# Scalar loads on another queue and a later second projection in the last chunk of an attention and gated feed-forward kernel

## The chip, the cores and the metric

The kernel runs on one core of a Trainium2 chip. The metric is the device time of one execution in microseconds (us); the times below are those of the kernel before, and the median of its runs is what the changed kernel is held against. The engines are named as in the profile: PE is TensorE (matmuls; PEld are its weight loads), DVE is VectorE, ACT is ScalarE, POOL is GpSimd, and SP is SyncE, which issues nearly all DMAs.

## The reference

Attention with a sliding window of 128 and 4 sink positions for 4 x 8 heads of 768 positions by 64, followed by a gated feed-forward block over all 3072 rows:

```python
def _attn_ref(q, k, v, n_sink, window):
    scores = scale * np.matmul(q, k.transpose(0, 1, 3, 2))
    keep = is_sink | in_window          # pos < n_sink, 0 <= rel < window
    scores = np.where(keep, scores, -1000000000.0)
    scores = scores - np.max(scores, axis=-1, keepdims=True)
    a = np.exp(scores)
    a = a / (np.sum(a, axis=-1, keepdims=True) + 1e-09)
    return np.matmul(a, v).astype(np.float32)

def _moe_ref(x, w_gate, w_val, w_out):
    gate = 1.0 / (1.0 + np.exp(-(x @ w_gate)))
    val = x @ w_val
    return (gate * val @ w_out).astype(np.float32)
```

`x` has 512 columns, `w_gate` and `w_val` are 512 x 1536, `w_out` is 1536 x 512. `n_sink` and `window` are two integers that the kernel reads from memory.

## The kernel before

**Work.** Attention runs in 96 units: one head, two tiles of 128 rows each. The first 16 units (`PLAIN`) multiply in plain float32; the later ones, and the feed-forward, split each operand into a high and a low part and sum three products of them. The weights arrive as pairs of 32-bit words and are decoded on DVE, ACT and POOL into high and low parts (`decode`). The low part of `w_out` (`wlo`) is written back to memory (`wol_d`) and read again per block into `wol`, two buffers in turn.

**Feed-forward.** The rows are cut into eight chunks (`MT`); the last one (`ci == 7`) has three tiles, 384 rows. For each of 12 blocks `f` of 128 hidden columns `feed_part` (line 1089) emits: the up projections, 12 matmuls into one PSUM tile `m` for the gate (weights `wgh`, `wgl`) and 12 into another for the value (`wvh`, `wvl`); `th` (a tanh on ACT, then a product on DVE); `gh` (its high part, on ACT or DVE) and `gl` (the rest, on POOL or DVE, helper `rest`); and the second projection `down`, nine matmuls `o<-woh,gh`, `o<-wol,gh`, `o<-woh,gl` for three output tiles, which accumulate over the blocks. After block 11 ACT halves each `o` into an output tile and SP sends it out.

**Order.** Nothing is placed by hand. Every step is an `Op` with a priority and one or more engines that could do it (`ways`). `Plan.run` walks them through a small model of the five queues (Q is SP's) and writes out one fixed order for each engine; an engine then works strictly through its row of instructions and stops at a wait. On PE, where nothing else is ready in the first stretch, the planner puts warming matmuls `m<-ident`. Priorities on PE are `pe = 10000 + ci + f / 12`: the gate of block `f` at `pe`, the value at `pe + 0.3 / 12`, `down` at `pe + 0.5 / 12`. So `down` of block `f` ranks ahead of both up projections of block `f + 1`, although it is passed over while its inputs are not surely there.

**Scalars.** `n_sink` and `window` are loaded by two DMAs at the head of SP's row (line 571). DVE turns them into the masks `am`, which the first unit needs.

**The way out.** A count of unusual inputs (`count<-bad,one` on PE, `flag` and `total` on DVE, lines 1197 to 1201) is loaded by every engine (`TENSOR_LOAD`, line 1203); if it is above zero, a slow general version runs, else every engine branches past that code (line 1204) to the end of the program.

Of the kernel before, what the change touches and what calls it, by code (L numbers as in the profile page):

```python
# [24 lines left out]
MT = ((2,2),(2,),(3,),(3,),(3,),(3,),(3,),(3,))  # L25
# [8 lines left out]
SCALP = -0.5  # L34
# [399 lines left out]
def kernel(  # L434
# [20 lines left out]
    DO = w_out.shape[1]  # L455
    NC = DM // 128
    NF = DF // 128
# [20 lines left out]
    plan = Plan()  # L478

    class InOrder:  # L480
# [9 lines left out]
    PE, V, A, G, Q = (  # L490
        InOrder(e) for e in (nc.tensor, nc.vector, nc.scalar, nc.gpsimd, nc.sync)
    )

    def vec(cols, fast=False):
        return 80 + (0.95 if fast else 1.25) * cols

    def act(cols, psum=False):
        return (48 if psum else 90) + 0.84 * cols

    def pool(cols):  # L500
        return 250 + 2.2 * cols

    def mac(cols):
        return max(cols * 13 / 12 / 2.4, 104.5) + 2.5

    def dma(prio, ns, fn, r=(), w=()):
        plan.op(prio, [("Q", 460, fn)], r, w, dma=ns)

    def copy(prio, cols, out, in_, r, w, psum=False):

        plan.op(
            prio,
            [
                ("A", act(cols, psum), lambda: A.copy(out=out(), in_=in_())),
                ("V", vec(cols, not psum), lambda: V.tensor_copy(out=out(), in_=in_())),
            ],
            r, w,
        )

    def rest(prio, cols, out, in0, in1, r, w, psum=False):  # L520

        plan.op(
            prio,
            [
                (
                    "G", pool(cols), lambda: G.tensor_tensor(
                        out=out(), in0=in0(), in1=in1().bitcast(F32), op=ALU.subtract
                    ),
                ),
                (  # L530
                    "V", vec(cols), lambda: V.tensor_tensor(
                        out=out(), in0=in0(), in1=in1().bitcast(F32), op=ALU.subtract
                    ),
                ),
            ][1 if psum else 0 :],
            r, w,
        )
# [13 lines left out]
    def tile(shape, dtype, tag, bufs, pool=None):  # L551
        return Tile(pool or p1, shape, dtype, tag, bufs)
# [15 lines left out]
    nums = tile([128, 10], I32, "nums", 1)  # L568
    mk = tile([128, 704], F32, "wst", BUFS["wst"], p2)

    for i, s in enumerate((n_sink, window)):
        dma(
            SCALP, 56.0, lambda i=i, s=s: Q.dma_start(
                out=nums()[:, 2 * i : 2 * i + 2],
                in_=s.bitcast(I32).rearrange("(o x) -> o x", o=1).broadcast_to([128, 2]),
            ), w=[(nums, i)],
        )

    def scalars():
# [481 lines left out]
    def feed(ci, g, parts):  # L1061

        O = []
        for p, T in enumerate(parts):
            for _ in range(T):
                j = len(O)
                O.append(
                    tile([128, DO], F32, f"o{j}", 1, ps)
                    if j < 3 else tile([128, DO], F32, "a", BUFS["a"], ps)
                )  # L1070
        for f in range(NF):
            j0 = 0
            for p, T in enumerate(parts):
                feed_part(ci, g, p if len(parts) > 1 else None, j0, T, f, O[j0 : j0 + T])
                j0 += T
        for j, acc in enumerate(O):
            ot = (
                tile([128, DO], F32, "qkT", BUFS["turned"]) if ci == len(MT) - 1 and j == 2
                else tile([128, DO], F32, "w2", BUFS["w2"])
            )  # L1080
            r = (g + j) * 128
            plan.op(
                -1000.0 + ci + 1,
                [("A", act(DO, True), lambda acc=acc, ot=ot: A.mul(out=ot(), in_=acc(), mul=0.5))],
                [acc], [ot],
            )
            dma(ci, 728.0, lambda ot=ot, r=r: Q.dma_start(out=out[r : r + 128], in_=ot()), [ot])

    def feed_part(ci, g, p, j0, T, f, O):
        W = T * 128  # L1090
        r0 = (g + j0) % RING
        xs = slice(r0 * 128, r0 * 128 + W)
        pr = -1000.0 + ci + f / NF
        pe = 10000.0 + ci + f / NF
        wgh, wgl, wvh, wvl, woh = wres[f]
        wol = tile([128, DO], F32R, f"wol{f % 2 if p is None else p}", BUFS["wol"])
        dma(
            pr, 728.0, lambda: Q.dma_start(out=wol().bitcast(F32), in_=wol_d[f]),
            [(WOL, f)] + ([] if f else [(XH, (NC - 1, r0 + T - 1))]), [wol, (LOADS, p)],
        )  # L1100
        th = tile([128, W], F32, "th", BUFS["th"])
        gh = tile([128, W], F32R, "gh", BUFS["g"])
        gl = tile([128, W], F32R, "gl", BUFS["g"])
        for i, (hi, lo) in enumerate(((wgh, wgl), (wvh, wvl))):
            m = Tile(MS, None, F32, "m", BUFS["m"])
            todo = [
                (c, j, w, x)
                for c in range(NC)
                for j, (w, x) in enumerate(((hi, XH), (hi, XL), (lo, XH)))
            ]  # L1110
            for s in range(UPS):
                part = todo[s * 12 // UPS : (s + 1) * 12 // UPS]

                def up(part=part, m=m):
                    for c, j, w, x in part:
                        PE.matmul(
                            m()[:, 0:W], lhsT=w()[:, c], rhs=x()[:, c, xs],
                            start=c == 0 and j == 0, stop=c == NC - 1 and j == 2,
                        )

                plan.op(
                    pe + 0.3 * i / NF, [("PE", len(part) * mac(W), up)],
                    [hi, lo] + [(x, (c, r0 + t)) for c, _, _, x in part for t in range(T)],
                    [m] if s else [m, th, (GROUPS, p)] if i == 0 else [m, gh, gl, (GROUPS, p)],
                )
            if i == 0:
                plan.op(
                    pr, [("A", act(W, True), lambda m=m: A.activation(
                        out=th(), in_=m()[:, 0:W], func=AF.Tanh, scale=0.5
                    ))],  # L1130
                    [m], [th],
                )
            else:
                plan.op(
                    pr, [("V", vec(W), lambda m=m: V.scalar_tensor_tensor(
                        out=th(), in0=th(), scalar=1.0, in1=m()[:, 0:W], op0=ALU.add,
                        op1=ALU.mult,
                    ))],
                    [m], [th],
                )  # L1140
        copy(pr, W, gh, th, [th], [gh])
        rest(pr, W, gl, th, gh, [th, gh], [gl])
        for j in range(T):

            def down(j=j):
                ts = slice(j * 128, j * 128 + 128)
                for i, (x, w) in enumerate(((gh, woh()[:, 0]), (gh, wol()), (gl, woh()[:, 0]))):
                    PE.matmul(
                        O[j](), lhsT=x()[:, ts], rhs=w,
                        start=f == 0 and i == 0, stop=f == NF - 1 and i == 2,  # L1150
                    )

            plan.op(
                pe + 0.5 / NF, [("PE", 3 * mac(DO), down)], [gh, gl, woh, wol], [O[j]]
            )

    decoding = iter(range(3 * NF))
# [95 lines left out]
```

## Time and profile before

| | us |
|---|---|
| runs | 796.38, 807.41, 798.26 |
| median | 798.26 |
| profiled execution | 798.38 |
| its span, first to last instruction | 796.7 |
| PE busy in the span | 773.8 (97%) |
| DVE, ACT, POOL busy | 513.4, 403.2, 437.5 |

The profiled execution has 1.7 us outside its span (798.38 less 796.7). All instructions of the plan are recorded under one line, 488, so they are told apart by the tiles that they write and read (`out<-in`). A busy share near 100% on PE says that PE is where the time is, but it includes the warming matmuls and stretches at a lower clock.

### The profile page before, as it was taken

What the parts mean: (1) busy time and instruction counts of PE and PEld (TensorE: products, weight loads), DVE (VectorE), ACT (ScalarE), POOL (GpSimd) and SP (SyncE); (2) the same over time, 40 slices, a digit from 0 to 9 for tenths busy, and PEclk for the clock granted to TensorE, in tenths of its full rate; (3) what the DMA queues carried; (4) which work ended last, traced back from release to release, by engine and by line L of the source; (5) the groups of instructions that cost most, each with busy time, mean ns of one, the idle gap of its engine ahead of it and who ended that gap; (6) DMA issues with size and microseconds to landing.
All of it is one profiled execution on the core that took longest, in us unless ns stands there. A gap on an engine that the chain in (4) does not pass through costs nothing. (4 is left out here: it accounts for less than half of the span.)

```text
span 796.7 us, 14763 instructions
## 1 busy us (share of the span) xinstructions
PE 773.8 (97%) x4540; PEld 702.8 (88%) x4540; DVE 513.4 (64%) x1550; ACT 403.2 (51%) x1190; POOL 437.5 (55%) x602
## 2 busy tenths in 40 slices
PE   7999999999999999999999999999999999999996
PEld 5677798878999999998999999999999999999995
DVE  5787798998799988899871388885861331111110
ACT  4786777766767767676640256664740210011001
POOL 3676798887667778668761267673751221111211
PEclk8999999999999999999999999999999999999999
DMA  5667777763645544444441235343311121113111
GB/s 162 198 190 207 191 213 253 231 201 115 192 126 151 149 107 122 119 116 112 142 113 40 57 104 133 104 129 111 92 45 42 41 79 40 40 40 92 39 42 57
DMA packets 98421, 94.33 MB, mean 118 GB/s; under 512 B 43168, under 2 KB 77984, under 8 KB 98336
## 3 DMA queue, kind: packets, MB, share of 16 engines
q1 hardware_dynamic: 98336, 93.32, 41.1%
q8 instruction: 38, 0.62, 0.3%
q14 instruction: 47, 0.39, 0.1%
HBM read 83.85 MB, written 9.44 MB: 117 GB/s over the span
## 5 line engine op out<-in xcount | busy, mean ns | idle before, releaser
L488 DVE SCALAR_TENSOR_TENSOR th<-th,m 128x384 f32<-128x384 f32 (+1 forms) x108 | 54.6, 505 | 184.3 <-PE m L488 182.9
L488 POOL TENSOR_TENSOR gl<-th,gh 128x384 fp32r<-128x384 f32 (+1 forms) x65 | 65.5, 1008 | 195.4 <-DVE gh L488 183.0
L488 ACT ACTIVATE th<-m 128x384 f32<-128x384 f32 (+1 forms) x108 | 49.1, 454 | 209.4 <-PE m L488 207.5
L488 POOL TENSOR_SCALAR_AFFINE_SELECT wt<-wt 128x512 fp32r<-128x512 f32 (+3 forms) x192 | 121.5, 633 | 42.6 <-DVE wt L488 24.2
L488 PE MATMUL m<-XH,wvh 128*128 128x384 f32 (+1 forms) x432 | 140.1, 324 | 0.4 <-ACT th L488 0.4
L488 PE MATMUL m<-XH,wgh 128*128 128x384 f32 (+1 forms) x432 | 140.3, 325 | 0.0
L488 PE MATMUL m<-XH,wvl 128*128 128x384 f32 (+1 forms) x432 | 137.7, 319 | 0.0
L488 PE MATMUL m<-XL,wvh 128*128 128x384 f32 (+1 forms) x432 | 137.6, 319 | 0.0
L488 PE MATMUL m<-XH,wgl 128*128 128x384 f32 (+1 forms) x432 | 137.5, 318 | 0.0
L488 PE MATMUL m<-XL,wgh 128*128 128x384 f32 (+1 forms) x432 | 137.3, 318 | 0.0
L488 PE MATMUL o<-woh,gh 128*128 128x512 f32 x276 | 113.0, 409 | 1.0 <-DVE total L1201 1.0
L488 PE MATMUL o<-woh,gl 128*128 128x512 f32 x276 | 109.5, 397 | 2.2 <-DVE gl L488 1.6
L488 PE MATMUL o<-wol,gh 128*128 128x512 f32 x276 | 108.8, 394 | 2.5 <-DMA wol<-wol_d 2.5
L488 ACT ACTIVATE P<-P,negm_all 128x132 f32<-128x132 f32 x192 | 77.2, 402 | 30.5 <-DVE negm_all L488 27.0
L488 PEld LDWEIGHTS m<-XH,wvh 128*128 128x128 f32 x432 | 81.7, 189 | 3.3 <-ACT th L488 0.6
L488 PEld LDWEIGHTS m<-XH,wgh 128*128 128x128 f32 x432 | 81.4, 189 | 2.1 <-issue 0.2
L488 PEld LDWEIGHTS m<-XL,wvh 128*128 128x128 f32 x432 | 81.8, 189 | 1.5
L488 PEld LDWEIGHTS m<-XL,wgh 128*128 128x128 f32 x432 | 81.5, 189 | 1.6
L488 PEld LDWEIGHTS m<-XH,wvl 128*128 128x128 f32 x432 | 81.7, 189 | 0.0
L488 PEld LDWEIGHTS m<-XH,wgl 128*128 128x128 f32 x432 | 81.3, 188 | 0.0
L488 PEld LDWEIGHTS o<-woh,gl 128*128 128x128 f32 x276 | 52.0, 188 | 16.6 <-DVE gl L488 3.5
L488 DVE CUSTOM_DVE_ANT_0 P<-a,am 128x132 f32<-128x132 f32 x192 | 56.2, 294 | 11.9 <-PE a L488 2.9
(115 smaller groups left out, 1619.5 us busy)
## 6 DMA issues: line engine op xcount, KB each, us to landing
wol<-wol_d SPq DMA_DIRECT2D x108, 256.0 KB, 2.7
qkT<-in_k_dram SPq DMA_DIRECT2D x120, 99.0 KB, 2.6
qkT<-in_q_dram SPq DMA_DIRECT2D x176, 64.0 KB, 2.4
wst<-in_moe_w_gate_dram SPq DMA_DIRECT2D x12, 512.0 KB, 4.3
wst<-in_moe_w_val_dram SPq DMA_DIRECT2D x12, 512.0 KB, 4.3
wst<-in_moe_w_out_dram SPq DMA_DIRECT2D x12, 512.0 KB, 4.2
vraw<-in_v_dram SPq DMA_DIRECT2D x64, 96.0 KB, 2.3
out_dram<-w SPq DMA_DIRECT2D x23, 256.0 KB, 2.5
```

Of the source, the lines that this page charges most:

```text
L488: return lambda *a, **kw: tc.keep_in_program_order(op(*a, **kw))
```

## The change

The two scalars are loaded by ACT's queue in place of SP's. In the last chunk `down` gets the priority `pe + 1.4 / 12`, which is behind both up projections of the next block (the next value projection is at `pe + 1.3 / 12`). In the last chunk's last block `gl` is computed by DVE alone: the fifth flag of `rest` strikes POOL off the list.

```diff
     for i, s in enumerate((n_sink, window)):
-        dma(
-            SCALP, 56.0, lambda i=i, s=s: Q.dma_start(
+        plan.op(
+            SCALP, [("A", 460, lambda i=i, s=s: A.dma_start(
                 out=nums()[:, 2 * i : 2 * i + 2],
                 in_=s.bitcast(I32).rearrange("(o x) -> o x", o=1).broadcast_to([128, 2]),
-            ), w=[(nums, i)],
+            ))], w=[(nums, i)], dma=56.0,
         )
...
         pe = 10000.0 + ci + f / NF
+        last = ci == len(MT) - 1
...
-        rest(pr, W, gl, th, gh, [th, gh], [gl])
+        rest(pr, W, gl, th, gh, [th, gh], [gl], last and f == NF - 1)
...
-                pe + 0.5 / NF, [("PE", 3 * mac(DO), down)], [gh, gl, woh, wol], [O[j]]
+                pe + (1.4 if last else 0.5) / NF, [("PE", 3 * mac(DO), down)], [gh, gl, woh, wol], [O[j]]
```

Since the planner decides step by step, the two loads' new place alters its choices from the first microseconds on, and the rows of all engines come out in another order along the whole program. Three places follow.

PE at the end of the last chunk, before: the last value projection (block 11), the count, and the `down` of block 11; `down` of block 10 (`woh10`) stands ahead of these rows.

```order
L488 MATMUL m0_90<-XL_83,wvh11_151 128x384
L488 MATMUL m0_90<-XH_82,wvl11_152 128x384
L1197 MATMUL count_10044<-bad_10036,one_10042 1x4
L488 MATMUL o00_9564<-woh11_153,gh1_10014 128x512
L488 MATMUL o00_9564<-wol10_9982,gh1_10014 128x512
L488 MATMUL o00_9564<-woh11_153,gl1_10016 128x512
```

The same place now: the last value projection is followed by the nine matmuls of block 10, of which the first three are shown.

```order
L488 MATMUL m1_91<-XL_83,wvh11_151 128x384
L488 MATMUL m1_91<-XH_82,wvl11_152 128x384
L488 MATMUL o00_9583<-woh10_148,gh1_9971 128x512
L488 MATMUL o00_9583<-wol00_9942,gh1_9971 128x512
L488 MATMUL o00_9583<-woh10_148,gl1_9976 128x512
```

And PE's last rows now: the count has moved behind the last matmul of `down`, directly ahead of the load of `total`.

```order
L488 MATMUL o20_9594<-woh11_153,gh0_10013 128x512
L488 MATMUL o20_9594<-wol10_9984,gh0_10013 128x512
L488 MATMUL o20_9594<-woh11_153,gl0_10018 128x512
L1198 MATMUL count_10046<-bad_10038,one_10044 1x4
L1204 TENSOR_LOAD total_10050
L1205 COMPARE_AND_BRANCH
```

SP at the end, before: the load of `total` stands ahead of the three last output DMAs.

```order
L488 DMA wol10_9982<-wol_d_93 128x512
L1203 TENSOR_LOAD total_10048
L1203 ISA x2
L488 DMA out_0_dram<-w21_10024 128x512
L488 DMA out_0_dram<-w20_10030 128x512
L488 DMA out_0_dram<-qkT2_10033 128x512
```

Now the load of `total` comes behind them.

```order
L488 DMA wol10_9984<-wol_d_93 128x512
L488 DMA out_0_dram<-w21_10026 128x512
L488 DMA out_0_dram<-w20_10032 128x512
L488 DMA out_0_dram<-qkT2_10035 128x512
L1204 TENSOR_LOAD total_10050
L1204 ISA x2
```

ACT at the start, before (`P` are the first units' weights: the rows with `negm_all` are the exponentials, those with `rs` alone as second input scale by the row sums; `w<-wst` begins the decoding of a gate and a value weight block):

```order
L488 ACT_TABLE_LOAD
L488 CAST vsp_84<-w20_190 96x512
L488 ACTIVATE P0_215,rs0_218<-P0_215,negm_all_80 128x132 x2
L488 ACTIVATE P1_230,rs1_234<-P1_230,negm_all_80 128x132
L488 ACTIVATE w21_241<-wst1_205 128x512
L488 ACTIVATE w20_248<-wst2_209 128x512
L488 ACTIVATE P0_215<-P0_215,rs0_218 128x128 x2
```

Now the two scalar loads stand ahead of the table load, and the first weight decoding stands ahead of three of the exponentials.

```order
L488 DMA nums0_156<-in_n_sink_dram 128x2
L488 DMA nums0_156<-in_window_dram 128x2
L488 ACT_TABLE_LOAD
L488 CAST vsp_84<-w20_179 96x512
L488 ACTIVATE P0_219,rs0_226<-P0_219,negm_all_80 128x132
L488 ACTIVATE w21_232<-wst1_196 128x512
L488 ACTIVATE P0_219,rs0_226<-P0_219,negm_all_80 128x132
L488 ACTIVATE P1_230,rs1_241<-P1_230,negm_all_80 128x132
L488 ACTIVATE w20_246<-wst2_200 128x512
L488 ACTIVATE P1_230,rs1_241<-P1_230,negm_all_80 128x132
L488 ACTIVATE P0_219<-P0_219,rs0_226 128x128
```

## Rows read from the trace of the kernel before

**Rows 1.** Busy time of the engines by stretch of the span. Columns: stretch, its length, then busy us (instructions) of PE, PEld, DVE, ACT and POOL, PE's granted clock as a share of full speed, the busy share of the DMA engines, GB/s.

```profile
0.00:50.00 50.00, 43.18 (x227) 31.52 (x228) 35.37 (x130) 32.08 (x93) 29.11 (x52) 0.93 0.61 181
50.00:100.00 50.00, 47.87 (x300) 39.10 (x299) 39.42 (x114) 36.54 (x107) 34.19 (x45) 0.97 0.69 198
100.00:200.00 100.00, 94.60 (x643) 84.61 (x643) 92.22 (x204) 72.06 (x191) 85.54 (x93) 1.00 0.66 201
200.00:786.00 586.00, 585.05 (x3365) 545.89 (x3364) 345.37 (x1101) 260.68 (x798) 287.70 (x414) 1.00 0.34 93
```

**Rows 2.** The timeline of the last blocks: start, duration, engine, line, operation, tiles; in brackets the idle time before it and what ended that. The first two rows are the first matmul of `down` of block 10 and the first of the value projection of block 11; the third is the last of that projection.

```profile
782.02 0.40 PE L488 MATMUL o<-woh,gh 128*128 128x512 f32 x1
...
784.11 0.33 PE L488 MATMUL m<-XH,wvh 128*128 128x384 f32 x1
...
786.05 0.34 PE L488 MATMUL m<-XH,wvl 128*128 128x384 f32 x1
...
786.49 0.56 DVE L488 SCALAR_TENSOR_TENSOR th<-th,m 128x384 f32<-128x384 f32 x1 [7.46 <-PE m L488]
...
787.08 0.36 DVE L488 CAST gh<-th 128x384 fp32r<-128x384 f32 x1
787.36 0.14 DVE L1201 TENSOR_REDUCE total<-flag 1x1 int32<-1x4 int32 x1
787.50 0.51 PE L488 MATMUL o<-woh,gh 128*128 128x512 f32 x1 [0.99 <-DVE total L1201]
787.61 1.00 POOL L488 TENSOR_TENSOR gl<-th,gh 128x384 fp32r<-128x384 f32 x1 [7.38 <-DVE total L1201]
...
788.67 0.50 PE L488 MATMUL o<-woh,gl 128*128 128x512 f32 x1 [0.44 <-POOLq L1204]
...
790.17 0.39 PE L488 MATMUL o<-woh,gl 128*128 128x512 f32 x1
```

**Rows 3.** The forms of `gl` and `gh` on single engines from 580 to 790 us: count, then min/median/max of one in ns, first and last start.

```profile
L488 DVE TENSOR_TENSOR gl<-th,gh x1: 547/547/547, 582.3 to 582.3; 128x384 fp32r<-128x384 f32 x1
...
L488 POOL TENSOR_TENSOR gl<-th,gh x32: 999/1012/1024, 589.9 to 787.6; 128x384 fp32r<-128x384 f32 x32
...
L488 ACT CAST gh<-th x1: 512/512/512, 581.4 to 581.4; 128x384 fp32r<-128x384 f32 x1
```

**Rows 4.** DMA issues of the reloaded low weights: number, size of one, median us from issue to landing.

```profile
wol<-wol_d SPq DMA_DIRECT2D x108, 256.0 KB, 2.7
```

**Rows 5.** The timeline behind PE's last matmul: ACT's last halving and SP's second and third output DMA (SPq is SP's sequencer; the duration is that of the issue).

```profile
790.59 0.60 ACT L488 ACTIVATE qkT<-o 128x512 f32<-128x512 f32 x1
...
790.57 1.54 SPq L488 DMA_DIRECT2D out_dram<-w  x1
792.15 0.43 SPq L488 DMA_DIRECT2D out_dram<-qkT  x1
```

**Rows 6.** All issues of output DMAs: min/median/max ns, first and last start.

```profile
L488 SPq DMA_DIRECT2D out_dram<-w x23: 332/362/1538, 200.1 to 790.6; - x23
```

**Rows 7.** The load of `total` (line 1203) and the branch past the general code (line 1204) on the sequencers: min/median/max ns, first and last start us. The semaphore row of an engine is the first instruction that it runs behind its branch; SP's eight wait for the last DMAs.

```profile
L1203 PEldq TENSOR_LOAD <-total x1: 488/488/488, 788.7 to 788.7; - x1
...
L1204 SPq EVENT_SEMAPHORE  x8: 17/17/17, 794.0 to 795.3; - x8
L1204 DVEq COMPARE_BRANCH  x1: 72/72/72, 788.2 to 788.2; - x1
...
L1204 PEldq COMPARE_BRANCH  x1: 3822/3822/3822, 789.3 to 789.3; - x1
L1204 DVEq EVENT_SEMAPHORE  x1: 21/21/21, 791.0 to 791.0; - x1
...
L1204 SPq COMPARE_BRANCH  x1: 45/45/45, 792.6 to 792.6; - x1
```

**Rows 8.** The timeline of the first 14 us on SP, ACT, DVE and PE.

```profile
0.80 0.40 SPq L488 DMA_DIRECT2D nums<-in_n_sink_dram  x1
1.72 0.56 SPq L488 DMA_DIRECT2D qkT<-in_k_dram  x1
...
4.70 0.24 DVE L488 CAST nums<-nums 128x2 f32<-128x2 uint32 x2 [2.15 <-DMA nums<-in_window_dram]
...
7.13 0.29 DVE L488 CUSTOM_DVE_ANT_0 P<-a,am 128x132 f32<-128x132 f32 x1
...
9.37 0.39 ACT L488 ACTIVATE P<-P,negm_all 128x132 f32<-128x132 f32 x1
11.13 0.70 ACT L488 ACTIVATE w<-wst 128x512 f32<-128x512 f32 x1 [1.28 <-DMA wst<-in_moe_w_gate_dram]
12.55 0.66 ACT L488 ACTIVATE w<-wst 128x512 f32<-128x512 f32 x1 [0.72 <-DMA wst<-in_moe_w_val_dram]
13.11 0.68 ACT L488 ACTIVATE P<-P,rs 128x128 f32<-128x128 f32 x2
...
13.55 0.77 PE L488 MATMUL a<-ident,P 128*128 128x128 f32 x2 [4.05 <-ACT P L488]
```

**Rows 9.** PE alone by stretch (busy us, instructions, granted clock, DMA share, GB/s), and the matmul that ended the wait ahead of the second of them.

```profile
12.40:19.20 6.80, 5.65 (x19) 0.50 0.56 170
...
84.10:87.40 3.30, 3.30 (x14) 0.50 1.05 289
...
83.61 0.50 PE L488 MATMUL o<-wol,gh 128*128 128x512 f32 x1 [1.34 <-DMA wol<-wol_d]
```

## The prediction

> **What bounds the kernel now.** I read the busy times by stretch first [rows 1]. From 200 to 786 us PE is busy for 585.05 of 586.00 us at full clock: there is nothing in that stretch for an order to win, and it holds nearly all of the last chunk. What can be won lies before 200 us, where PE stands still or is slow, and behind 786 us. The end is read from the timeline [rows 2]. The last value projection issues its last matmul at 786.05; matmuls of that width follow each other every 0.175 us here (12 of them from 784.11 to 786.05 and on to 786.22), so PE could go on at 786.22. It starts `down` of block 11 at 787.50, does two matmuls, waits for POOL's `gl` until 788.67 and starts its ninth at 790.17. The reason is a chain with nothing beside it: `th` on DVE until 787.05, `gh` until 787.44, `gl` on POOL from 787.61 to 788.61. The nine matmuls of block 10, from 782.02 to 784.11, were spent earlier. Behind PE's last matmul, which ends at 790.56, ACT halves the last tile (790.59 to 791.19), SP issues its DMA at 792.15 [rows 5], the wait for landings ends at 795.3 [rows 7], and the span at 796.7: 6.1 us from PE's end to the span's end.
>
> **The late second projection.** With `down` of block 10 behind the last value projection, as the order shows, its nine matmuls (784.11 - 782.02 = 2.09 us, or 0.232 each) fill the gap. The work is the same and only the gap goes. Without waits the last matmul would start at 786.22 + 8 x 0.232 = 788.08, against 790.17: **-2.09 us**. This holds if the chain stays under its cover. Counted from 786.22, the cover ends at 2.09 for `gh`, and at 2.09 + 2 x 0.232 = 2.55 for `gl`, which the third matmul needs. `th` is ready at 0.83 (787.05). A step between engines cost 0.17 before (787.44 to 787.61). The planner has put the last `gh` on ACT, 0.51 [rows 3]: 0.83 + 0.17 + 0.51 = 1.51. `gl` on DVE takes 0.55: 1.51 + 0.17 + 0.55 = 2.23, plus a step to PE some 2.35. It fits with 0.2 us to spare. In the other eleven blocks PE had no gap [rows 1], so the later `down` wins nothing there and costs nothing either: POOL's 1.01 [rows 3] has 24 up matmuls (4.2 us) as cover. The slot of `wol` comes free one projection later, but its next reader follows 10 us behind, and a reload takes 2.7 [rows 4].
>
> **The last rest on VectorE.** On POOL `gl` would end at 1.51 + 0.17 + 1.01 = 2.69, against the 2.55 at which it is needed. So this edit is worth 0.1 to 0.3 us of the 2.09, beneath the new cover; alone it would have been worth 1.01 - 0.55 = 0.5.
>
> **The way out.** The order shows two moves that the diff doesn't: the count runs behind PE's last matmul, and SP loads `total` behind its three output DMAs. Let E be the end of PE's last matmul. The DMA chain is the longest before: E + 6.1. One piece of it is odd: the second output DMA took 1.54 us to issue, against a median of 0.36 [rows 6], and held the third from 791.19 to 792.15. If it doesn't come again there, that chain ends at 0.63 (ACT) + 0.03 + 3.15 (792.15 to 795.3) + 1.4 (to the span's end) = E + 5.2, a gain of 0.9. But now the flag starts at E as well. From the end of the last up matmul (786.39) to `total` (787.50) it took 1.1 us before, with `th` and `gh` queued on DVE ahead of parts of it, so 0.5 to 1.1 now. PE's load of it takes 0.49 and its branch took 3.82 [rows 7]; by these the branch is over at E + 1.1 + 0.49 + 0.1 + 3.82 = 5.5, and with 1.4 behind it the end is at E + 6.9, a loss of 0.8. I take less, since of the 3.82 us PE was still multiplying for 1.28 (789.28 to 790.56); 2.5 are left, and DVE took 2.8 from its branch at 788.2 to its next instruction at 791.0. With 2.7 the branch is over at 4.4 and the end is at 5.8. So between -0.9 and +0.8 I choose **-0.3**, from the row of the engine that stood idle when it branched.
>
> [...]
>
> **The scalars on ACT.** SP's row begins 1.72 - 0.80 = 0.92 us earlier [rows 8]. Followed through, little of it arrives. The first reduction on DVE (7.13) waits for the masks, these for the landing of `window` (4.70), and ACT can issue that no earlier than SP did: the first unit's scores are earlier, its exponentials are not. If ACT's issues are slower or the table load behind them delays them, the masks come later, but ACT's next exponentials now stand behind the first weight decoding, which would come to 11.13 - 0.92 = 10.2, so some 1.5 us of lateness (10.2 less the first reduction's 7.13, the exponential's 0.58 and what lies between) is hidden, and what is beyond that costs its full size. Then the new row of ACT: decoding to 10.9, two exponentials at 0.58 each (9.37, and with its read of the sum to 9.85, is such a step; 0.58 is between starts) to 12.1, the second decoding to 12.8, an exponential to 13.4, the scaling: before it began at 13.11 and let PE go at 13.55. So PE's wait of 4.05 us ends at about the same time, 13.7. Between a full gain of 0.92 and a loss as large I take **0**.
>
> **The rest of the program.** The planner's choices differ from there on. PE has the same matmuls and 71 warming ones for 69. Whether PE waits more or less before 200 us can't be read from an order. Its price can be read from one event: PE waited 1.34 us for `wol` at 83.61, and then ran at half clock (1.2 GHz) from 84.1 to 87.4 [rows 9], which loses another 1.65: 3.0 us in all. The other such stretch, 12.4 to 19.2, followed the wait of 4.05 us. So the term is 0, with -3 and +3 as ends: one such event more or less.
>
> **Sum.** -2.09 - 0.3 + 0 + 0 = -2.4 against the profiled execution's own 798.38 (span 796.7 and 1.7 around it), which lies 0.12 above the median of 798.26. That gives **796.0 us**, 0.3% under the median.
>
> **The rivals.**
> *Another waiting of PE is added* (slower than before). The reshuffled row has one more event of the kind at 83.61, in the stretch before 200 us: 796.0 + 3.0 = 799.0, and 1.1 more, 800.1, if the way out is at its bad end as well. It decides from a loss of 2.3 us on, which is what the end gives against the median. For it: in that stretch DVE and POOL are busy for 92.22 and 85.54 of 100 us [rows 1], so a step placed badly isn't made up. Against: the planner's rules are the same.
> *An event goes.* SP's earlier start or another order removes the wait at 13.55 or the one at 83.61 with its half clock: 796.0 - 3.0 = 793.0. For it: all of SP's early loads are 0.92 earlier. Against: ACT's new row, above.
> *The way out eats the gain.* [...] In words of rows: PE's branch takes as long as it did before, though no matmul is left under it.
> *The change doesn't do what it says* (the chain outlasts its cover, say ACT's `gh` comes a microsecond late): at most the old gap comes back, 798.4 at the end; the order shows the matmuls in place, so I give this little.
>
> **How the numbers follow.** The forecast (794.5 to 797.0) gets 0.45; an event that goes (791.5 to 794.5) 0.2; the way out (797.0 to 797.6) 0.1; another waiting (797.6 to 801.5) 0.22; the last rival and anything else 0.03. The range from 791.8 to 800.4 leaves out about 0.15 at both ends. A 2% change, which is about what a measurement of this kernel tells from none, would mean 782.3 or 814.2; to get there five such events would have to come or go, and the two ways together get 0.03: faster 0.01, same 0.97, slower 0.02.
>
> **What the changed profile would show.** Right: nine `o` matmuls between the last `m<-XH,wvl` and block 11, no wait of PE at `o` there, and the last `o` starting some 1.86 us (8 x 0.232) behind the last block's first. The count behind it, and 5.2 to 6.1 us from PE's end to the span's end. The masks at about 4.7 us as before, and the first weight decoding near 10.2. Wrong: a wait of PE for ACT's `gh`; a branch of 3.8 us on PE behind `total`; half-clock stretches in other places or lengths than the two of [rows 9], which would decide more than the three edits together.

## The result: slower by 0.85%, and where the time went

The changed kernel took 805.66 us at the median against 798.82 in the runs made beside it. The ratio is 1.0085 with a 95% interval of 1.0065 to 1.0105. Here and below the ratios leave out disturbed runs, among them one of 2651 us of the changed kernel that no trace explains, and the medians leave out none, so that the two disagree by up to 0.2%. Beside the experiments the kernel before took 799.4 to 800.5 us at the median. The forecast was 796.0, 0.3% under the kernel before, with a range that ended at 800.4: the sign was wrong and the time lies outside the range. The profiled execution took 803.41 us (span 801.4), 5.0 us above the one of before.

The end of the last chunk does what it was meant to do. This is the timeline of the changed kernel from the last value projection on, the lines that answer to [rows 2]:

```profile
790.80 0.34 PE L488 MATMUL m<-XH,wvl 128*128 128x384 f32 x1
790.98 0.40 PE L488 MATMUL o<-woh,gh 128*128 128x512 f32 x1
...
791.25 0.55 DVE L488 SCALAR_TENSOR_TENSOR th<-th,m 128x384 f32<-128x384 f32 x1 [5.72 <-PE m L488]
...
791.83 0.52 ACT L488 CAST gh<-th 128x384 fp32r<-128x384 f32 x1 [2.19 <-DVE th L488]
...
792.38 0.56 DVE L488 TENSOR_TENSOR gl<-th,gh 128x384 fp32r<-128x384 f32 x1 [0.58 <-ACT gh L488]
...
793.08 0.40 PE L488 MATMUL o<-woh,gh 128*128 128x512 f32 x1
...
794.94 0.39 PE L488 MATMUL o<-woh,gl 128*128 128x512 f32 x1
...
795.37 0.60 ACT L488 ACTIVATE qkT<-o 128x512 f32<-128x512 f32 x1
795.49 0.15 DVE L1200 CAST flag<-count 1x4 int32<-1x4 f32 x1 [2.55 <-PE count L1198]
795.67 0.14 DVE L1202 TENSOR_REDUCE total<-flag 1x1 int32<-1x4 int32 x1
...
795.99 0.33 SPq L488 DMA_DIRECT2D out_dram<-qkT  x1
```

From the last value projection's last start to the last `o`'s start are 4.14 us with 18 second projections, and they were 4.12 with 9 (786.05 to 790.17 in [rows 2]): the gap of two microseconds is gone. But the same work, all up to the last nine matmuls, is done 6.86 us later than before: 793.08, against 786.22. So PE came late to the last chunk, and the three places of the diff aren't where it lost the time. By stretch, the lines that answer to [rows 1]:

```profile
0.00:50.00 50.00, 43.34 (x210) 30.62 (x211) 31.53 (x121) 31.90 (x92) 26.55 (x48) 0.86 0.59 174
50.00:100.00 50.00, 47.49 (x295) 38.74 (x294) 38.57 (x119) 32.70 (x98) 32.30 (x45) 0.97 0.64 185
100.00:200.00 100.00, 94.33 (x647) 84.68 (x646) 90.30 (x197) 75.30 (x200) 83.12 (x89) 1.00 0.67 205
200.00:786.00 586.00, 583.97 (x3352) 543.04 (x3351) 333.30 (x1067) 289.34 (x856) 287.25 (x406) 1.00 0.34 93
```

PE's busy time hardly differs from [rows 1] in any of them, and that is the trap: a warming matmul and a matmul at half clock are busy time too (6.6 us of the one between 50 and 150 us, 3.35 of 3.40 us at the second half clock, both below). What differs is the granted clock of the first 50 us (0.86 for 0.93) and the number of matmuls (210 for 227 there, 3352 for 3365 behind 200 us). The half clock shows in the windows of PE alone, which answer to [rows 9], as a granted share of 0.50. No row has it in GHz; what the traces have for the prediction's 1.2 is the step from one 128x256 matmul to the next, 0.213 us there (256 columns, 1.2 per ns) and 0.12 at full clock. The half clock lasted 13.70 us at the start instead of 6.80, and as long as before around 93 us.

```profile
11.30:25.00 13.70, 11.00 (x34) 0.50 0.46 139
93.20:96.60 3.40, 3.35 (x15) 0.50 0.37 96
```

The order alone does not set the length of the stretch at the start. The run of the scalar loads alone (below) has the same rows up to the last chunk, and there it lasted as long as in the kernel before; that execution had another 6.8 us at half clock from 156.3 us on, at a wait of 3.8 us, where the changed kernel's trace has none.

```profile
13.00:19.80 6.80, 5.42 (x19) 0.50 0.39 114
```

The warming matmuls are another sign. They stand only where the planner had nothing else ready for PE. Here is their group between 50 and 150 us (count, then busy us and mean ns of one), in the kernel before:

```profile
L488 PE MATMUL m<-ident 128*128 128x128 f32 x22 | 3.6, 284 | 0.2
```

and in the changed kernel:

```profile
L488 PE MATMUL m<-ident 128*128 128x128 f32 x36 | 6.6, 307 | 0.2 <-ACT th L488 0.2
```

From the start of each such group to the next real matmul the timeline gives 2.2 us in 6 places before and 7.1 us in 10 places now. Over the whole span these gaps grew from 26.0 to 30.0 us.

To place the 6.86 us, take for every other matmul the time from its start to the next one's, less the median of its kind at full clock in the two traces (the account of start times, below). Ahead of 200 us the matmuls at half clock lost 1.8 us more than before and all others 2.6 us less, so that with the 4.0 of the gaps the changed kernel is 3.2 us behind there. The other 3.6 us are lost between 200 us and the end of the up projections, where neither kernel has a warming matmul or half clock: 8.4 us of such delays, against 4.8. Of 0.1 us and more there are 22 with 5.1 us together, where before there were five with 1.8. They are short. From one start of an up projection to the next are about 0.17 us; here they are 0.80:

```profile
374.99 0.34 PE L488 MATMUL m<-XH,wvl 128*128 128x384 f32 x1
375.79 0.39 PE L488 MATMUL a<-kh,qs 128*128 128x260 f32 x1 [0.46 <-DVE wt L488]
```

Busy time and the list of waits hold little of them. This part follows the order: in the five traces that have these rows there (the changed kernel and four of the experiments below) it is 8.1 to 9.1 us, and in the four that have the rows of the kernel before 4.7 to 4.8.

The list of PE's waits names what was late (us in total, times, longest). In the changed kernel:

```profile
PE a L488 <- ACT P L488: 4.2, 1, 4.2
PE a L488 <- DVE negm_all L488: 3.6, 3, 2.8
PE a L488 <- ACT xr L488: 2.0, 1, 2.0
```

The first was there before [rows 8]. The other two are new at that length. Both end a chain that begins with a load. The longer of them in the timeline of the changed kernel (in brackets the idle time of the engine and what ended it):

```profile
152.04 0.38 SPq L488 DMA_DIRECT2D wst<-in_moe_w_val_dram  x1
...
157.04 0.67 ACT L488 ACTIVATE wst<-wst 128x512 int32<-128x512 uint8 x1 [3.64 <-DMA wst<-in_moe_w_val_dram]
...
157.60 0.68 ACT L488 ACTIVATE P<-P,rs 128x128 f32<-128x128 f32 x2
158.18 0.39 ACT L488 CAST gh<-th 128x256 fp32r<-128x256 f32 x1
...
158.61 0.42 DVE L488 TENSOR_TENSOR gl<-th,gh 128x256 fp32r<-128x256 f32 x1 [3.08 <-ACT gh L488]
...
159.39 0.47 PE L488 MATMUL a<-wt,vhl 128*128 128x512 f32 x1 [2.82 <-DVE negm_all L488]
```

ACT stood 3.64 us at a decoding step whose load came 5.0 us after its issue; the scaling of `P` and the `gh` that PE and DVE needed were queued behind it. The other is of the same build: at 90.81 ACT had stood 2.65 us at the split of `v` (`vhl<-vraw`), and PE went on at 93.25 after 1.96 us.

### The profile page after: what moved, and what is told of

Same layout as the page of the kernel before. It is cut to its first block, busy times and chain, and to the rows that moved or that the text cites. A ratio compares the mean times of both kernels' runs of the same rounds, so it can differ in the third digit from the quotient of the medians.

```text
span 801.4 us, 14738 instructions
## 1 busy us (share of the span) xinstructions
PE 778.6 (97%) x4544; PEld 705.2 (88%) x4544; DVE 495.1 (62%) x1505; ACT 432.1 (54%) x1250; POOL 430.2 (54%) x587
## 4 chain that ended last, share of the span: by engine, by line
PE 76%; DVE 11%; DMA 6%; ACT 3%; issue 2%; SPq 1%; POOL 1%; DVEq 0%; POOLq 0%; ACTq 0%
PE m L488 43%; PE o L488 20%; PE a L488 12%; DVE w L488 3%; DMA wst<-in_moe_w_val_dram 2%; DMA wst<-in_moe_w_gate_dram 1%; SPq L488 1%; DVE P L488 1%; DVE a L488 1%; DVE gl L488 1%; DMA wol<-wol_d 1%; DVE wt L488 1%; DMA vraw<-in_v_dram 1%; DMA qkT<-in_k_dram 1%; DVE vhl L488 1%
## 5 line engine op out<-in xcount | busy, mean ns | idle before, releaser
L488 POOL TENSOR_TENSOR gl<-th,gh 128x384 fp32r<-128x384 f32 (+1 forms) x62 | 61.7, 995 | 177.0 <-ACT gh L488 175.7
L488 POOL TENSOR_SCALAR_AFFINE_SELECT wt<-wt 128x512 fp32r<-128x512 f32 (+3 forms) x192 | 119.3, 622 | 54.8 <-DVE wt L488 29.5
L488 ACT CAST gh<-th 128x384 fp32r<-128x384 f32 (+1 forms) x93 | 44.6, 479 | 107.1 <-DVE th L488 107.0
```

The costliest lines, as they stand in the source:

```text
L488: return lambda *a, **kw: tc.keep_in_program_order(op(*a, **kw))
```

## The experiments

The theory after this reading: the edits are worth what was forecast or nothing, and the new order that the planner made from them costs some 8 us. The rivals: ACT's issuing of the loads costs it; or the end costs it; or two badly placed waits do, which would be bad luck of this one order.

**Which part of the change.** First the scalar loads alone, planned and issued as in the change, with the end as it was.

> The scalar loads on ACT's queue alone; the late second projection and the last rest on DVE are undone. Its rows equal those of the changed kernel up to the last chunk. Theory 'order' (the rows as the planner re-wrote them starve PE before 200 us; the end of the change saves its 2.1 us): the kernel before + 9 us, ratio about 1.011. Theory 'queue' (ACT's issuing of the two loads itself delays the start): the same here. Theory 'end' (the late second projection and the way out cost the 7 us): within 1 us of the kernel before, ratio 1.000.

Measured: 805.19 us, ratio 1.0068 [1.0041, 1.0095]. The sign and most of the loss are in this part. It came out lower than the 1.011 that theory 'order' expected: the 2 us that the end saves do not show between the timed runs of this kernel and of the change.

Then the rest of the change, on the old place of the loads:

```diff
+        last = ci == len(MT) - 1
-        rest(pr, W, gl, th, gh, [th, gh], [gl])
+        rest(pr, W, gl, th, gh, [th, gh], [gl], last and f == NF - 1)
-                pe + 0.5 / NF, ...
+                pe + (1.4 if last else 0.5) / NF, ...
```

> The late second projection and the last rest on DVE alone; the scalars stay on SP's queue. Its rows equal those of the kernel before up to the last chunk. Theories 'order' and 'queue': 2 us under the kernel before, ratio 0.9975. Theory 'end': 5 to 7 us above it, ratio 1.007.

Measured: 797.86 us, ratio 0.9984 [0.9953, 1.0015]; the profiled span is 794.0 against 796.7 before. The rows before the end are those of before, and the last `o` starts 4.14 us behind the last value projection, with nine more second projections in between:

```profile
783.06 0.34 PE L488 MATMUL m<-XH,wvl 128*128 128x384 f32 x1
783.23 0.40 PE L488 MATMUL o<-woh,gh 128*128 128x512 f32 x1
...
787.20 0.39 PE L488 MATMUL o<-woh,gl 128*128 128x512 f32 x1
```

The trace also shows by how much two executions of the same rows can differ: PE ends this projection 0.9 us earlier than the moved nine matmuls account for (783.06 against 786.05 - 2.09 = 783.96). So the end saves what the timeline said, some 2 us in the trace; the timed runs alone can't tell 0.2% from nothing.

Next, who issues the loads. Here the planner still counts them to SP, so that the rows are those of before, and only the instruction goes to ACT's queue:

```diff
-            SCALP, 56.0, lambda i=i, s=s: Q.dma_start(
+            SCALP, 56.0, lambda i=i, s=s: A.dma_start(
```

> The planner places the two loads as before, on SP's row, but ACT issues them: every row is that of the kernel before, except that the two DMAs stand at the head of ACT's row and SP's row begins with the loads of k and q. Theory 'order': within 1 us of the kernel before, ratio 0.999 to 1.001 (no more than 0.9 us of gain from SP's earlier start). Theory 'queue': the kernel before + 7 to 9 us, ratio 1.01.

Measured: 799.74 us, ratio 1.0013 [0.9979, 1.0048]. And the reverse: the planner counts them to ACT, and SP issues them ahead of its row:

```diff
+            SCALP, [("A", 460, lambda i=i, s=s: Q.dma_start(
...
+        o.head = True
...
+        order.sort(key=lambda x: x[0] is None or not x[0].head)
```

> The opposite: the planner places the two loads on ACT as the change does, but SP issues them at the head of its row; all other rows are those of the first kernel of this call (scalars alone). Theory 'order': as that kernel, the kernel before + 9 us, ratio 1.011, perhaps 1 us more for SP's later start. Theory 'queue': within 1 us of the kernel before.

Measured: 807.54 us, ratio 1.0087 [1.0051, 1.0123]. The queue that issues the loads costs nothing that can be measured, that is, less than 0.5%. The order that comes of planning them elsewhere costs the 0.7 to 0.9%.

**The two waits at late loads.** In the changed kernel's order the decoding step that waited at 157 us was moved behind the scaling of `P` and the `gh` that stood behind it on ACT:

```diff
+        acts = [x for x in order if x[1] == "A"]
+        later([acts[254]], acts[257])
```

> The changed kernel with one instruction moved in one row: ACT's decoding step wst<-wst, on which ACT stood for 3.64 us at 153.4 to 157.0 in the changed kernel's profile (its weight block had not landed), now stands behind the two scalings of P and the gh cast that it held up. Theory 'waits at late loads' (in the new order ACT reaches some decoding steps before their weights have landed, and what stands behind them starves DVE and PE): PE's wait of 2.8 us at 156.6 goes, the changed kernel less 2 to 3 us, ratio against the kernel before 1.005 to 1.006. Theory 'spread' (the new order loses a little everywhere, and a wait that goes comes back at the next place): the same as the changed kernel, 1.0085.

Measured: 805.55 us, ratio 1.0046 [1.0009, 1.0083]. The wait that was aimed at is gone from PE's list:

```profile
PE a L501 <- ACT P L501: 4.8, 1, 4.8
PE a L501 <- ACT xr L501: 2.2, 1, 2.2
PE a L501 <- DVE negm_all L501: 1.6, 5, 0.5
```

But PE comes to its last nine matmuls at 792.88, only 0.2 us earlier than in the changed kernel (793.08):

```profile
792.88 0.40 PE L501 MATMUL o<-woh,gh 128*128 128x512 f32 x1
```

By the account of start times both traces lose 4.1 to 4.3 us between 150 and 175 us, here in shorter waits, the longest 0.8 us. So in the trace the wait came back at the next places, as theory 'spread' has it. The timed runs lean the other way, by 0.4% in the ratio's point value, but its interval overlaps that of the change.

Then the other one as well: the split of `v`, its low part on POOL and a decoding step behind the copy `xr<-a`.

```diff
+        low = next(x for x in order if x[0] in acts[136][0].after and x[1] == "G")
+        later([acts[136], low, acts[137]], acts[141])
```

> As the run before, and at 88 us as well: ACT's vhl cast, which waited 2.65 us for the load of v, and the decoding step behind it now stand behind the xr copy on which PE waited (with POOL's part of vhl behind that too). Theory 'waits at late loads': both of PE's long waits go, the changed kernel less 4 to 5 us, ratio 1.002 to 1.004. Theory 'spread': 1.0085.

Measured: 804.0 us, ratio 1.0039 [1.0008, 1.0071]. Both waits are gone from their places, but a new one has come at 118 us, again behind a step whose load came late (this time a decoding step on DVE):

```profile
PE a L503 <- ACT gh L503: 2.0, 1, 2.0
```

The kernel is still slower than before. By the point values of the ratios the two waits are about half of the loss (0.85% to 0.39%), but the intervals of the two overlap that of the change and other waits stand in their place, so the share is not settled.

**Is it this order, or any other?** The kernel before with one figure of the planner changed, the time it assumes for issuing each of the two loads: 470 in place of 460 ns. The loads stay on SP and nothing else is edited.

```diff
-        dma(
-            SCALP, 56.0, lambda i=i, s=s: Q.dma_start(
+        plan.op(
+            SCALP, [("Q", 470, lambda i=i, s=s: Q.dma_start(
...
-            ), w=[(nums, i)],
+            ))], w=[(nums, i)], dma=56.0,
```

> The kernel before with nothing changed but the planner's figure for the two scalar loads, 470 ns in place of 460; they stay at the head of SP's row. All engines' rows come out in another order from the first microseconds on. Theory 'any new order' (each re-planning gives another order, whose time differs by up to 1% either way, whatever caused it): off the kernel before by 2 to 8 us. Theory 'ACT' (only the loads' new place makes the order worse): within 1.5 us of the kernel before.

Measured: 806.35 us, ratio 1.0077 [1.0047, 1.0107]. The same with 400 ns:

> The same with 400 ns in place of 460. Theory 'any new order': off the kernel before by 2 to 8 us, on either side. Theory 'ACT': within 1.5 us of it.

Measured: 806.6 us, ratio 1.0091 [1.0061, 1.0121]. And with 420:

> The kernel before with the planner's figure of an issue of the two loads at 420 in place of 460 ns, nothing else; SP issues them. A third new order that no edit of the work asks for. Theory that the order before is an unusually good one among those the planner gives: 1.005 to 1.010. Rival, that new orders fall on both sides and the two others were chance: 0.995 to 1.003.

Measured: 806.51 us, ratio 1.0099 [1.0073, 1.0125]. The traces of the kernels planned with 400 and with 420 have the same rows on every engine. So the run with 420 is not the third new order that was expected, but the second one measured again, and the two times agree. Two new orders that no edit of the work asks for cost as much as the change does. By the account of start times they lose 5 to 10 us ahead of 200 us and at most 0.5 us behind it, so not in the same places as the change.

The marker of the changed kernel is in both: 32 warming matmuls between 50 and 150 us with 470, 33 and 34 with 400 and 420, where before has 22. Such a count also depends on when PE comes to them: the PE row of the changed kernel, 36 there, has 44 and 52 in the two runs with the longest half clock at the start (both waits moved, and SP issuing). This is the group in the kernel planned with 470,

```profile
L488 PE MATMUL m<-ident 128*128 128x128 f32 x32 | 5.2, 284 | 1.5 <-DVE th L488 1.5
```

and in the second-projection run above, which keeps the old rows:

```profile
L488 PE MATMUL m<-ident 128*128 128x128 f32 x22 | 3.6, 284 | 0.2
```

The waits of PE fall in other places each time. With 420 they are, the one at the start first:

```profile
PE a L488 <- ACT P L488: 4.5, 1, 4.5
PE o L488 <- DMA wol<-wol_d: 4.1, 4, 1.6
PE a L488 <- DVE wt L488: 2.2, 2, 1.8
PE a L488 <- POOL P L488: 1.6, 1, 1.6
PE a L488 <- DVE P L488: 1.5, 1, 1.5
```

**Does the planner place the readers of loads too early?** It lets a reader start 750 ns behind the end of a transfer. With 1500, in the changed kernel and in the kernel before:

```diff
-                        end = dma_free + 750
+                        end = dma_free + 1500
```

> The changed kernel, with the planner's figure for the time from a transfer's end to its readers' start at 1500 in place of 750 ns, so that ACT's and POOL's rows place readers of a load later. Theory that readers placed too early (the two waits at 90.7 and 156.3 us) are the cause: both waits go, 1.000 to 1.003. Rival that any order other than the one before costs this much, by waits wherever they fall: 1.006 to 1.010, with other waits.

Measured: 808.13 us, ratio 1.0086 [1.0041, 1.013].

> The kernel before with the same figure of 1500 in place of 750 ns, and no other edit. Theory of readers placed too early: not slower than before, 0.995 to 1.002. Rival that the order before is an unusually good one: 1.005 to 1.010.

Measured: 801.62 us, ratio 1.0017 [0.9988, 1.0046]. The first of the two fits the rival, the second the theory. In the changed kernel the later figure helps nothing: it costs the same with other waits (`wol` 3.8 us in 3 waits, two kinds of `th` 3.3), and 42 warming matmuls. (Some of that time is outside the span, 3.5 us against 2.0 in the changed kernel's trace, for a reason that stays open.) So the readers' places are not the cause by themselves. In the kernel before it gives the one new order of three that is not clearly slower, though it too has 34 warming matmuls in that stretch; it has no half clock between 24 and 790 us. An early marker alone does not give the sum, then.

**All three edits, old rows.** The end as in the change, the loads issued by ACT, and the planner's account of the loads as it was.

> The rows of the kernel before, kept as they were planned, with ACT issuing the two scalar loads, and the late second projection and the last rest on DVE at the end: all three edits without a new plan of the first 700 us. Theory (the new order costs some 9 us, the end saves 2): 0.997 to 0.998 of the time before, some 2 us less. Rival (the end's saving was lost again, or ACT's issue costs something that a single run hid): 1.000 or more.

Measured: 796.61 us, ratio 0.9982 [0.9952, 1.0011]. The profiled span is 794.7 us. This beats the changed kernel by some 1% and agrees with the forecast of 796.0, which is the sum without a cost of the new order. Against the kernel before it is not told from no change.

## Why the prediction was wrong

**What bounds the kernel** was read half right. The gap at the end was real. But "nothing in that stretch for an order to win", said of 200 to 786 us, was taken to mean that there was nothing to lose there either, and about half of the 6.86 us was lost there. [rows 1] can't say it: busy time hides short delays between matmuls (8.4 us of them in the changed kernel, with PE busy for 583.97 of 586.00), and ahead of 200 us it holds the warming matmuls and those at half clock.

**The late second projection**, -2.09: right. All work up to block 11 to the last `o` takes 2 us less in the change and in the run of this part alone. `th` was ready 0.82 us behind the last projection (0.83 forecast), `gh` at 1.37 (1.51) and `gl` at 1.96 (2.23 to 2.35), against a cover of 2.55. The difference is the step between engines: 0.03 us here, where I had taken the 0.17 from `gh` to POOL.

**The last rest on DVE**, 0.1 to 0.3 of the above: too much by the same step. From ACT's `gh` to POOL's `gl` the step is mostly 0.08 in this trace, so on POOL it would have ended at 1.37 + 0.08 + 1.01 = 2.46, just under the cover as well. That was not run by itself.

**The way out**, -0.3: wrong, it is about 0. From PE's end (795.33) to the span's end are 6.0 us, against 6.1 before. The 1.54 us issue did not come again (the last issue took 0.33), but PE's branch did not shrink. These are the rows of the changed kernel that answer to [rows 7] (min/median/max ns, first and last start):

```profile
L1205 PEldq COMPARE_BRANCH  x1: 3558/3558/3558, 796.7 to 796.7; - x1
L1205 DVEq COMPARE_BRANCH  x1: 72/72/72, 796.8 to 796.8; - x1
...
L1205 DVEq EVENT_SEMAPHORE  x1: 21/21/21, 797.4 to 797.4; - x1
L1205 PEldq EVENT_SEMAPHORE  x1: 51/51/51, 800.4 to 800.4; - x1
```

I had taken 1.28 us off PE's 3.82, because it was still multiplying, and set 2.7 by DVE's 2.8. PE's took 3.56 with no matmul beside it, and DVE's was over in 0.6. The rival that kept PE's whole branch had the mechanism right, but not its loss of 0.8: `total` was there 0.5 us behind PE's end (795.67 + 0.14) and not 1.1, and the branch itself was 0.26 shorter. SP's eight waits for the last DMAs were over at 798.5, 3.2 us behind PE's end. Only one of its semaphores behind the program's end is long, 1.515 us from 798.93, and it ended at 800.4, as PE's semaphore did:

```profile
L1249 SPq EVENT_SEMAPHORE  x10: 17/28/1515, 798.6 to 801.3; - x10
```

So PE's branch was the last to end, and the DMAs were not. With the old rows and the new end it was worse: 6.4 us (PE's end at 787.59, span 794.0), and there DVE's next instruction came later than PE's (793.0 against 792.6). Something stands between the branch and an engine's next instruction, of a size that differs by engine (in the changed kernel 0.2 us on POOL, 0.6 on DVE, 3.6 on PE); what it is, no row shows.

**The scalars on ACT**, 0 ± 0.92: right. The masks come as before (the casts of the scalars at 4.72 against 4.70), the first weight decoding at 10.32 (10.2 forecast), and PE's first long wait ends at 13.45 (13.7 forecast, 13.55 before). Issued by ACT with the old rows the loads cost nothing (1.0013).

**The rest of the program**, 0 with ±3: this is the step that failed. It measured +6.86, the lateness at the last nine matmuls: with -2.09 for the end and 0 for the way out that makes the +4.7 by which the span grew. Three things were wrong in it. It was taken as symmetric: one event more or less. But the order before seems to be one at the good end of what this planner gives: of three other orders, got by figures of the planner without an edit of the work, two cost 0.8 to 1.0%, one 0.2% (not told from nothing), and none was faster. The price of a re-plan was sized by one event of 3 us, where a new order moves the gaps everywhere: ten groups of warming matmuls between 50 and 150 us for six, and 22 delays of 0.1 us and more behind 200 us for five. And I compared the warming matmuls by their total, 71 against 69 steps of two instructions, and found nothing in it. Where they stand tells more, 36 against 22 instructions between 50 and 150 us, though it doesn't tell of the loss behind 200 us.

*Another waiting of PE is added* was the rival that came true in its sign. Its mechanism was one more event, a wait with half clock behind it, for 3.0 us; what came is spread over many places and has twice that price, so that 805.66 lies above its end of 801.5 too. It had a chance of 0.22. As the order's rows already differed on every engine from the first microseconds, it should have been the forecast or near it. The prediction also says that a measurement tells about 2% from none; this one told 0.85% from none (1.0065 to 1.0105).

What stays open: what the lost microseconds are made of in an order. Warming gaps, half clock, and waits at late inputs share them differently in each kernel, two of the waits were removed and gave back some 4 us by the point values of the ratios but not in the trace of the first, and no single rule of the planner was found that makes the difference. That the order before is an unusually good one is an inference from few others, not something that a run shows.

## What to carry to other kernels

Where a planner sets the order, an edit to an early step is two changes: the edit, and a new order for everything behind it. Measure them apart by keeping the rows and moving only the instruction, and re-plan the kernel with a figure that means nothing to see what a new order costs by itself; here none of three re-plans was faster, so that cost was not centred on zero. Compare the orders of such re-plans too: two figures can give the same one.

For an order that can be read ahead of a run, look where the fillers stand and not only how many there are, but take it as a hint: one order here had as many early fillers as those that cost 0.8 to 1.0%, and was not clearly slower. PE's busy share hides fillers, half clock and short delays alike (it is 97% in both kernels here): compare when the same piece of work is done. And before a difference between two traces is put down to the order, look at a second trace of the same rows.

## What was unexpected of the hardware

PE's branch out of the program took 3.82 us in the kernel before, where PE multiplied beside it for 1.28, and 3.56, 3.56 and 3.66 in the changed kernel, the run of the end alone and that of all three edits on the old rows, where it multiplied nothing: these four traces differ by 0.3 us at most. DVE's next instruction came 0.6 us behind its branch in the changed kernel, 2.9 in the kernel before, and 3.9 in the run of the end alone (789.1 to 793.0). That may go with the rows: the run of all three edits, which has those of the end alone on DVE, had 4.1 (789.6 to 793.7). Why, no row shows.

How long the stretch at half clock at the start lasts differs between executions of the same rows. With the rows that the change has there it was 6.8 us (scalar loads alone), 13.7 (changed kernel and one wait moved), 23.9 (both waits moved) and 27.3 (SP issuing the loads), where PE's wait for `P` there was 4.6, 4.2, 4.8, 3.6 and 5.7 us; with 400 and 420, the same order twice, it was 10.2 and 13.7, with waits of 3.9 and 4.5. In all four traces with the rows of before it was 6.8, so the order may still make a long one likelier. It starts at 12.4 us in the kernel before, at 11.3 in the changed kernel and at 13.0 in the run of the scalar loads alone. Of 34 executions of the kernel before beside the first experiments, the mean granted clock was 0.974 to 0.997; the 18 at 0.99 or more took 799.5 us on average and the 16 below it 804.1. So one trace is one draw of the half clock, and the times hold many.
